# Loading and attending batch 0 in two row ranges, with fp32 rows below 256 by hardware DMA and a replanned opening

## Chip, cores, metric

One core of a Trainium2 chip (trn2). The metric is the device time of one execution in microseconds; medians over several runs are given. "Ratio" always means a kernel's time against the kernel before, run on the same chip in the same rounds.

## The reference, cut

Causal attention with 16 extra "beacon" keys and values that every query sees, then a two-layer feed-forward with ELU.

```python
B, H, S, Nb, D = 8, 8, 576, 16, 64          # all fp32
k_all = concat([beacon_k, k], axis=2); v_all = concat([beacon_v, v], axis=2)
scores = q @ k_all^T / 8;  causal mask on the S keys (beacons never masked)
a = softmax(scores);  attn = a @ v_all       # -> x: 4608 x 512
h = x @ w_in                                 # 512 x 2048
out = where(h > 0, h, exp(min(h, 0)) - 1) @ w_out
```

## The kernel before: the parts that matter here

The order of all instructions is written by hand for batches 0 to 2; a regular loop does the rest, one 512-token tile of the feed-forward beside the attention of one batch. Short names of the steps: `T` transposes q and k on TensorE, `cq`/`ck` copy them out, `S` a quarter of a head pair's scores, `x` their exponential on ScalarE, `m` the mask, `L` the row sums, `W` the value product, `n` the reciprocal by logarithm and exponential, `M` the scaling, `F` first matrix, `e r g` the ELU, `G` second matrix, `warm` multiplications of zeros that keep TensorE's clock up.

```python
# q and k: cast to bf16 by the software DMA queue (GpSimd), six rows per partition
def load_qk(b, h0, h1):
    for src, dst in ((q, st[b][0]), (k, st[b][1])):
        nc.gpsimd.dma_start(out=dst[:, h0:h1, :, :]..., in_=src[b, h0:h1, :, :]...)
# ... beacon keys on the two hardware queues
for b in range(B):
    (nc.sync if b % 2 == 0 else nc.scalar).dma_start(out=bk32[NB*b:NB*(b+1), :, :], in_=beacon_k[b]...)
# ... keys stand in chunks j of 128 rows; the last one has 80: kc = [128, 128, 128, 128, 80]
def quad(b, g, qa, qe, t, half, first):      # row sums (ones) or value product of four heads
    pcs = [...]                              # the pieces (chunk j, queries a to e, column c) of this query range
    for n, (j, a, e, c) in enumerate(pcs):
        for i in range(4):
            nc.tensor.matmul(out=t[32*i:32*(i+1), a-qa:e-qa],
                lhsT=ones[0:kc[j], :] if half is None else v16[0:kc[j], j, h, 32*half:32*(half+1)],
                rhs=ets[b, p][0:kc[j], i % 2, c:c+e-a], ...)
# ... four matmuls of one piece lie beside each other in four 32-column parts of the array
```

In batches 1 to 7, `L` and `W` of queries 0 to 511 call `quad` with five pieces, so a group of 20 matmuls; the last piece is chunk 4 with the 16 queries 496 to 511.

The softmax here doesn't subtract the row's maximum and nothing guards it: scores larger than these inputs give would overflow.

## Time and profile before

| | kernel before |
|---|---|
| median, 3 runs | 361.54 us (360.62 to 362.31) |
| profiled execution | 367.16 us, span on the core 365.5 us |
| TensorE busy | 96% of the span |

The profile's page gives busy times, then 40 equal slices; the chain of waits follows back from the last instruction what released each step. The lines are shown in the prediction. One number of the table deserved more attention than I gave it: the profiled execution took 5.6 us longer than the median.

### The profile page before, as it was taken

How to read it: one execution, taken by the hardware profiler on the slowest of the kernel's cores; microseconds unless marked ns; L12 is line 12 of the kernel's file. 1: busy time of each engine (PE TensorE's matmuls, PEld its weight loads, DVE VectorE, ACT ScalarE, POOL GpSimd, SP SyncE). 2: the span in 40 equal slices, each digit the busy share in tenths (PEclk: the TensorE clock that was granted, in tenths of full speed). 3: DMA queues.
4: the chain of work that ended last, by engine and by line, in shares of the span. 5: the costliest groups of instructions: out<-in, count | busy, mean ns of one | idle time of the engine just before them, and what ended most of it. 6: DMA issues, size and time to landing. Idle time of an engine off the chain costs nothing.

```text
span 365.5 us, 9406 instructions
## 1 busy us (share of the span) xinstructions
PE 350.7 (96%) x3944; PEld 172.6 (47%) x3944; DVE 252.8 (69%) x615; ACT 218.9 (60%) x345; POOL 97.8 (27%) x130
## 2 busy tenths in 40 slices
PE   7979999979999999999999999999999999999995
PEld 3546765533445444544454454445444444444442
DVE  3444883766987877777777878786868677677731
ACT  1997988665765776677566756776576433333300
POOL 8867447387194008400500050000000000000000
PEclk9997999998999999999999999999999999999999
DMA  8999999999999639973954294432000001001012
GB/s 119 170 197 168 181 200 146 102 162 152 169 92 152 83 102 96 164 82 90 100 67 60 61 117 76 64 63 63 29 32 30 30 30 57 29 30 58 29 64 81
DMA packets 124299, 34.69 MB, mean 95 GB/s; under 512 B 111969, under 2 KB 118625, under 8 KB 124257
## 3 DMA queue, kind: packets, MB, share of 16 engines
q0 software_dynamic: 93600, 18.49, 62.6%
q1 hardware_dynamic: 30080, 15.47, 21.6%
q8 instruction: 31, 0.51, 0.6%
q10 hardware_dynamic: 576, 0.13, 0.2%
q14 instruction: 12, 0.09, 0.1%
HBM read 37.22 MB, written 15.34 MB: 144 GB/s over the span
## 4 chain that ended last, share of the span: by engine, by line
PE 83%; ACT 9%; DVE 5%; issue 1%; DMA 1%; ACTq 0%; DVEq 0%
PE hps L434 34%; PE ops L465 32%; PE sc L278 7%; PE lt L315 5%; ACT et L288 3%; PE ut L315 3%; DVE xT L385 2%; ACT rl L351 1%; ACT rl L348 1%; DVE gt L456 1%; DMA bk_83<-in_beacon_k_dram 1%; DVE r L449 1%; ACT e L444 1%; ACT qk_97 L257 1%; PE w_161 L200 0%
## 5 line engine op out<-in xcount | busy, mean ns | idle before, releaser
L434 PE MATMUL hps<-xT,w_in_81 128*128 128x512 f16 (+1 forms) x640 | 151.1, 365 | 1.3 <-DVE gt L456 1.2
L465 PE MATMUL ops<-w_out_82,gt 128*128 128x512 f16 x576 | 145.3, 379 | 0.0
L444 ACT ACTIVATE e<-hps 128x512 f32<-128x512 f32 x144 | 85.4, 598 | 62.9 <-PE hps L434 62.4
L288 ACT ACTIVATE et<-sc 128x832 f16<-128x832 f32 x128 | 103.6, 873 | 17.6 <-PE sc L278 17.6
L456 DVE TENSOR_TENSOR gt<-hps,r 128x512 f16<-128x512 f32 x144 | 99.6, 691 | 5.4
L449 DVE TENSOR_SCALAR r<-e 128x512 f16<-128x512 f32 x144 | 65.3, 454 | 32.2 <-ACT e L444 30.8
L465 PEld LDWEIGHTS <-gt 128*128 128x128 f16 x576 | 55.8, 98 | 66.6 <-issue 0.6
L434 PEld LDWEIGHTS <-w_in_81 128*128 128x128 f16 x640 | 58.6, 99 | 60.6 <-issue 7.9
L304 DVE TENSOR_TENSOR et<-et,triu 128x256 f16<-128x256 f16 (+3 forms) x164 | 40.4, 270 | 27.9 <-ACT et L288 27.5
L472 DVE COPY osb<-ops 128x512 f32<-128x512 f32 x36 | 24.6, 682 | 10.2 <-PE ops L465 10.2
L494 POOL DMA_DIRECT2D qkd<-in_k_dram x20 | 20.2, 1362 | 3.7 <-DMA v_1733<-in_v_dram 2.4
L385 DVE TENSOR_TENSOR xT<-lt,rl 128x448 f16<-128x448 f32 (+6 forms) x28 | 10.6, 419 | 14.6 <-ACT rl L351 14.6
L494 POOL DMA_DIRECT2D qkd<-in_q_dram x20 | 18.8, 1053 | 3.8 <-DMA w_out_82<-in_moe_w_out_dram 3.4
L348 ACT ACTIVATE rl<-lt 128x512 f32<-128x512 f32 (+1 forms) x15 | 9.0, 603 | 16.7 <-PE lt L315 16.7
L348 ACT ACTIVATE rl<-ut 128x64 f32<-128x64 f32 x14 | 3.1, 223 | 23.0 <-DVE xT L385 23.0
L315 PEld LDWEIGHTS <-ones 128*32 128x32 f16 (+1 forms) x624 | 10.9, 97 | 8.7 <-issue 5.8
L351 ACT ACTIVATE rl<-rl 128x512 f32<-128x512 f32 (+2 forms) x30 | 13.8, 459 | 0.9
L385 DVE TENSOR_TENSOR xT<-ut,rl 128x448 f16<-128x448 f32 (+6 forms) x28 | 10.5, 416 | 4.5 <-PE ut L315 3.7
L200 PE MATMUL w_161<-zero 64*128 64x512 bf16 (+1 forms) x36 | 11.4, 440 | 1.3 <-DVE zero L152 1.3
L315 PE MATMUL lt<-et,ones 128*32 128x512 f16 (+7 forms) x320 | 12.3, 286 | 0.0
L140 POOL DMA_DIRECT2D w_in_81<-in_moe_w_in_dram x16 | 8.5, 542 | 4.2 <-DMA kst<-in_k_dram 1.0
L123 POOL DMA_DIRECT2D v_4331<-in_beacon_v_dram x1 | 0.5, 532 | 33.0 <-PE ut L315 33.0
(116 smaller groups left out, 221.7 us busy)
## 6 DMA issues: line engine op xcount, KB each, us to landing
...
```

The source lines that it names most:

```text
L278: nc.tensor.matmul(out=s[:, h, a - c0:e - c0], lhsT=t[D * h:D * (h + 1), 1, P * j:P * (j + 1)], rhs=t[D * h:D * (h + 1), 0, NB + qa + a - ...
L288: nc.scalar.activation(out=ets[b, p][:, :, GW * g:GW * (g + 1)], in_=sc[b, p, g][:, :, 0:GW], func=AFT.Exp, bias=0.0, scale=SCALE)
L304: nc.vector.tensor_tensor(out=o, in0=o, in1=triu[0:kc[j], :, t0:t0 + e - a], op=ALU.mult)
L315: nc.tensor.matmul(out=t[32 * i:32 * (i + 1), a - qa:e - qa], lhsT=ones[0:kc[j], :] if half is None else v16[0:kc[j], j, h, 32 * half:32 * ...
L385: nc.vector.tensor_tensor(out=x_tile(k)[:, cc, tok - TT * k:to - TT * k], in0=u[:, o:o + to - tok], in1=r[:, o:o + to - tok], op=ALU.mult)
L434: nc.tensor.matmul(out=h[:, n_, :], lhsT=w_in16[:, cc, P * fc:P * (fc + 1)], rhs=xt[k][:, cc, a - TT * k:e - TT * k], start=(cc == 0), sto ...
L444: nc.scalar.activation(out=eb[t, i], in_=flat(hp[t, i]), func=AFT.Exp, bias=0.0, scale=1.0)
L449: nc.vector.tensor_scalar(out=rb[t, i], in0=eb[t, i], scalar1=1.0, scalar2=1.0, op0=ALU.min, op1=ALU.subtract)
L456: nc.vector.tensor_tensor(out=flat(gt), in0=flat(hp[t, i]), in1=rb[t, i], op=ALU.max)
L465: nc.tensor.matmul(out=ob[t, tb_], lhsT=gts[t, fc][:, P * tb_:P * (tb_ + 1)], rhs=w_out16[:, fc, :], start=(fc == 0), stop=(fc == NFC - 1))
L472: nc.vector.tensor_copy(out=osb, in_=ob[t, tb_])
L494: nc.gpsimd.dma_start(out=st[b][i][s0:s0 + S // 4], in_=src[b, :, s0:s0 + S // 4].rearrange("h s d -> s h d"))
```

## The change

Its intent: rows 0 to 255 of batch 0 get their own loads, transposes and attention, so that the feed-forward can start on the first 256 tokens early. q and k below 256 come as fp32 over the hardware queues (no cast) and are transposed as fp32 matmuls against an identity; the rest follows as bf16 over the software queue. All copies of batch 0 go to VectorE, and the order of steps and loads is replanned. The core of the diff (cuts marked):

```diff
+    def load_qa(h0, h1):
+        for eng, src, dst in ((nc.sync, q, qa0[0]), (nc.scalar, k, qa0[1])):
+            eng.dma_start(out=dst[:, h0:h1, :, :]..., in_=src[0, h0:h1, 0:CUT, :]...)
+    def load_qb():                       # rows 256 and up, nc.gpsimd.dma_start, bf16
...
     for b in range(B):
         (nc.sync if b % 2 == 0 else nc.scalar).dma_start(out=bk32[...], in_=beacon_k[b]...)
+        if b in (1, 3):
+            load_qa(4 * (b // 2), 4 * (b // 2) + 4)
...
         for n, (j, a, e, c) in enumerate(pcs):
+            nk = min(kc[j], NB + e - P * j)
             for i in range(4):
                 nc.tensor.matmul(...
-                    lhsT=ones[0:kc[j], :] if half is None else v16[0:kc[j], j, h, ...],
-                    rhs=ets[b, p][0:kc[j], i % 2, c:c + e - a],
+                    lhsT=ones[0:nk, :] if half is None else v16[0:nk, j, h, ...],
+                    rhs=ets[b, p][0:nk, i % 2, c:c + e - a],
...
-    warm.12 bt bk cb.0.0 cb.0.3 cb.0.2 cb.0.1 cb.1.0 warm.3 T.0.0 cb.1.1 cb.1.3 cq.0.0 ck.0.0
+    warm.6 ld.qkA0 bt bk TA.0.0 cb.0.0 cb.0.1 cb.0.2 ld.qkA1 cb.0.3 cA.0.0 TA.0.1 TA.0.2 cb.1.0
... (the whole hand-written order is new)
```

`nk` is the number of key rows of a chunk that any of the piece's queries may see. Rows 0 to 255 need it, since only 16 rows of v's chunk 2 are loaded by then. But `quad` serves all batches: for chunk 4 and queries 496 to 511, `nk` is 16 where it was 80.

More of the change, by code (lines that the diff above doesn't have):

```diff
@@ L108, in new_stage @@
     def new_stage(b):
-        qst = stage.tile([PR, H, R, D], BF16, tag="qst")
-        kst = stage.tile([PR, H, R, D], BF16, tag="kst")
-        st.setdefault(b, [None] * 3)[0:2] = [qst, kst]
+        ts = [stage.tile([P, 2048], FP32, tag=tag, name=tag) for tag in ("qst", "kst")]
+        st.setdefault(b, [None] * 3)[0:2] = [
+            t[0:PR, 0:H * R * D // 2].bitcast(BF16).rearrange("p (h r d) -> p h r d", h=H, r=R) for t in ts]
     def load_qk(b, h0, h1):
@@ L118, in load_qk, with load_v @@
             )
-    def load_v(b, js):
+    RA, RB = CUT // P, 4
+    PB = (S - CUT) // RB
+    NA = H * RA * D
+    q0 = [stage.tile([P, NA + H * RB * D // 2], FP32, tag=tag, name=tag) for tag in ("qst", "kst")]
+    qa0 = [t[:, 0:NA].rearrange("p (h r d) -> p h r d", h=H, r=RA) for t in q0]
+    qb0 = [t[0:PB, NA:].bitcast(BF16).rearrange("p (h r d) -> p h r d", h=H, r=RB) for t in q0]
+    def load_qa(h0, h1):
+        for eng, src, dst in ((nc.sync, q, qa0[0]), (nc.scalar, k, qa0[1])):
+            eng.dma_start(
+                out=dst[:, h0:h1, :, :].rearrange("p h r d -> p h (r d)"),
+                in_=src[0, h0:h1, 0:CUT, :].rearrange("h (p r) d -> p h (r d)", r=RA))
+    def load_qb():
+        for src, dst in ((q, qb0[0]), (k, qb0[1])):
+            nc.gpsimd.dma_start(
+                out=dst.rearrange("p h r d -> p h (r d)"),
+                in_=src[0, :, CUT:S, :].rearrange("h (p r) d -> p h (r d)", r=RB))
+    def load_v(b, js, j_from=0, n_last=None):
         if js[0] == 0:
@@ L125, in load_v @@
         for j in js:
-            r0 = NB if j == 0 else 0
-            n = kc[j] - r0
+            r0 = NB if j == 0 else j_from if j == js[0] else 0
+            r1 = n_last if n_last and j == js[-1] else kc[j]
+            k0 = P * j - NB
             nc.gpsimd.dma_start(
-                out=st[b][2][r0:r0 + n, j, :, :],
-                in_=v[b, :, ilo[j]:ilo[j] + n, :].rearrange("h s d -> s h d"),
+                out=st[b][2][r0:r1, j, :, :],
+                in_=v[b, :, k0 + r0:k0 + r1, :].rearrange("h s d -> s h d"),
             )
@@ L159 @@
         nc.vector.memset(t[:, 1, SK:P * NKC], 0.0)
+    for t in qks[0:NP]:
+        nc.vector.memset(t[:, 1, NB + CUT:P * ((NB + CUT + P - 1) // P)], 0.0)
+    identf = konst.tile([P, P], FP32)
     identb = konst.tile([P, P], BF16)
     triu = konst.tile([P, 2, P], FP16)
-    bkst = konst.tile([P, H, D], BF16)
-    bkT = konst.tile([P, NP, P], BF16)
-    new_stage(0)
-    load_qk(0, 0, 2)
+    bkT = konst.tile([P, NP * P], BF16)
+    make_identity(nc, identf)
     make_identity(nc, identb)
-    load_qk(0, 2, 4)
     nc.gpsimd.memset(triu, 1.0)
@@ L173 @@
     )
-    load_qk(0, 4, 6)
-    load_qk(0, 6, 8)
-    new_stage(1)
-    load_v(0, [0, 1, 2])
-    load_v(0, [3, 4])
-    load_qk(1, 0, H // 2)
-    load_wi(0, 1024)
-    load_wi(1024, 2048)
-    load_qk(1, H // 2, H)
     op = {}
@@ L206, in bt @@
     def bt():
-        nc.vector.tensor_copy(out=bkst, in_=bk32)
-        tb.append(bank("hps", BF16, "tb"))
+        tb.append(bank("hps", name="tb"))
         for p in range(NP):
             nc.tensor.transpose(
-                out=tb[0][:, P * p:P * (p + 1)], in_=bkst[:, 2 * p:2 * p + 2, :], identity=identb)
+                out=tb[0][:, P * p:P * (p + 1)], in_=bk32[:, 2 * p:2 * p + 2, :], identity=identf)
     @step
     def bk():
-        nc.vector.tensor_copy(out=bkT, in_=tb[0][:, 0:NP * P])
+        nc.vector.tensor_copy(out=bkT, in_=tb[0])
@@ L217, with transposes @@
     tps, qkT, sc, ets = {}, {}, {}, {}
     seq = [0]
-    @step
-    def T(b, p):
-        if b == 0 and p < 3:
-            tps[b, p] = bank("hps", BF16, "tq"), bank("hps", BF16, "tk")
-            dsts = tps[b, p]
-        else:
-            tps[b, p] = psum.tile([P, 2, 1024], BF16, tag="S", name="tp")
-            dsts = tps[b, p][:, 0, :], tps[b, p][:, 1, :]
-        for dst, src in zip(dsts, st[b]):
-            for r in range(R):
-                for h in range(2):
-                    nc.tensor.transpose(
-                        out=dst[D * h:D * (h + 1), PR * r:PR * (r + 1)],
-                        in_=src[:, 2 * p + h, r, :],
-                        identity=identb[0:PR, 0:PR],
-                    )
+    def transposes(dsts, srcs, p, nr, w, ident):
+        for dst, src in zip(dsts, srcs):
+            for r in range(nr):
+                for h in range(2):
+                    o = dst[D * h:D * (h + 1), w * r:w * (r + 1)]
+                    x = src[:, 2 * p + h, r, :]
+                    if ident is identf:
+                        nc.tensor.matmul(
+                            out=o, lhsT=x, rhs=ident, start=True, stop=True, skip_group_check=True)
+                    else:
+                        nc.tensor.transpose(out=o, in_=x, identity=ident[0:w, 0:w])
@@ new lines, in halves, with TA, TB @@
+    def halves(t, n):
+        return t[:, 0:n], t[:, n:2 * n]
+    @step
+    def TA(b, p):
+        tps["A", p] = bank("hps", name="ta")
+        transposes(halves(tps["A", p], CUT), qa0, p, RA, P, identf)
+    @step
+    def TB(b, p):
+        tps["B", p] = psum.tile([P, 2, 1024], BF16, tag="S", name="tbb")[:, 0, :]
+        transposes(halves(tps["B", p], S - CUT), qb0, p, RB, PB, identb)
+    def T(b, p):
+        tps[b, p] = psum.tile([P, 2, 1024], BF16, tag="S", name="tp")
+        transposes((tps[b, p][:, 0, :], tps[b, p][:, 1, :]), st[b], p, R, PR, identb)
@@ L237, in cb, with cA, cB @@
+    op["T"] = T
+    @step
+    def cA(b, p):
+        nc.vector.tensor_copy(
+            out=qkT[b, p][:, :, NB:NB + CUT].rearrange("c i (p r) -> c i p r", r=RA),
+            in_=tps["A", p].rearrange("c (i r p) -> c i p r", i=2, r=RA))
+    @step
+    def cB(b, p):
+        nc.vector.tensor_copy(
+            out=qkT[b, p][:, :, NB + CUT:SK].rearrange("c i (p r) -> c i p r", r=RB),
+            in_=tps["B", p][:, 0:2 * (S - CUT)].rearrange("c (i r p) -> c i p r", i=2, r=RB))
     @step
@@ L240, in cb @@
         seq[0] += 1
-        nc.vector.tensor_copy(out=qkT[b, p][:, 1, 0:NB], in_=bkT[:, p, NB * b:NB * (b + 1)])
+        nc.vector.tensor_copy(out=qkT[b, p][:, 1, 0:NB], in_=bkT[:, P * p + NB * b:P * p + NB * (b + 1)])
     @step
@@ L251, in ck @@
             return
-        if b == 0 and p < 3:
-            nc.scalar.copy(
-                out=t[:, 1, NB:SK].rearrange("c (p r) -> c p r", r=R),
-                in_=tps[b, p][1][:, 0:S].rearrange("c (r p) -> c p r", r=R))
-        else:
-            nc.scalar.copy(
-                out=t[:, :, NB:SK].rearrange("c i (p r) -> c i p r", r=R),
-                in_=tps[b, p][:, :, 0:S].rearrange("c i (r p) -> c i p r", r=R))
-    @step
-    def cq(b, p):
-        nc.vector.tensor_copy(
-            out=qkT[b, p][:, 0, NB:SK].rearrange("c (p r) -> c p r", r=R),
-            in_=tps[b, p][0][:, 0:S].rearrange("c (r p) -> c p r", r=R))
+        nc.scalar.copy(
+            out=t[:, :, NB:SK].rearrange("c i (p r) -> c i p r", r=R),
+            in_=tps[b, p][:, :, 0:S].rearrange("c i (r p) -> c i p r", r=R))
     def S_(b, p, g):
@@ L316, in quad @@
                     out=t[32 * i:32 * (i + 1), a - qa:e - qa],
-                    lhsT=ones[0:kc[j], :] if half is None else v16[0:kc[j], j, h, 32 * half:32 * (half + 1)],
-                    rhs=ets[b, p][0:kc[j], i % 2, c:c + e - a],
+                    lhsT=ones[0:nk, :] if half is None else v16[0:nk, j, h, 32 * half:32 * (half + 1)],
+                    rhs=ets[b, p][0:nk, i % 2, c:c + e - a],
                     start=(first and n == 0), stop=(n == len(pcs) - 1), skip_group_check=True)
@@ L323, in L @@
     @step
-    def L(b, g):
-        if g == "A":
+    def L(b, *g):
+        if g[0] == "A":
             t = bank("ops", name="la")
@@ L330, in L @@
                 quad(b, i, 0, CUT, t[:, CUT * i:CUT * (i + 1)], None, i == 0)
-            lt[b, g] = t
-        elif g == "B":
-            t = psum.tile([P, 2, 512], FP32, tag="S", name="lt")
-            for i in range(2):
-                quad(b, i, CUT, S, t[:, i, 0:S - CUT], None, True)
-            lt[b, g] = t[:, :, 0:S - CUT]
+            lt[b, *g] = t
+        elif g[0] == "B":
+            t = lt[b, *g] = bank("ops", name="lb")[:, 0:S - CUT]
+            quad(b, g[1], CUT, S, t, None, True)
         else:
             t = psum.tile([P, 2, 512], FP32, tag="S", name="lt")
-            quad(b, g, 0, Q1, t[:, 0, :], None, True)
-            lt[b, g], ut[b, g, 0] = t[:, 0, :], t[:, 1, :]
+            quad(b, g[0], 0, Q1, t[:, 0, :], None, True)
+            lt[b, *g], ut[b, *g, 0] = t[:, 0, :], t[:, 1, :]
     @step
@@ L345, in n @@
         w = src.free_size()
-        rl = rls[b, *g] = attn.tile([P, 640], FP32, tag="rl", name="rl")
+        rl = rls[b, *g] = attn.tile([P, 512], FP32, tag="rl", name="rl")
         dst = rl[:, 0:w]
-        nc.scalar.activation(
-            out=dst.rearrange("p (g c) -> p g c", g=2) if len(src.shape) == 3 else dst,
-            in_=src, func=AFT.Ln, bias=0.0, scale=1.0)
+        nc.scalar.activation(out=dst, in_=src, func=AFT.Ln, bias=0.0, scale=1.0)
         nc.scalar.activation(out=dst, in_=dst, func=AFT.Exp, bias=0.0, scale=-1.0)
@@ L398, in M @@
             g, half = i
-            scale_out(b, 2 * g + half, CUT, S, ut[b, "B", g, half][:, 0:S - CUT],
-                      rls[b, "B"][:, (S - CUT) * g:(S - CUT) * (g + 1)])
+            scale_out(b, 2 * g + half, CUT, S, ut[b, "B", g, half][:, 0:S - CUT], rls[b, "B", g][:, 0:S - CUT])
         elif g == "R":
@@ L480, in wo, with ld @@
     @step
-    def wo(i):
-        load_wo(i)
+    def ld(x):
+        i = x[-1]
+        if x.startswith("win"):
+            load_wi(DF // 2 * int(i), DF // 2 * (int(i) + 1))
+        elif x.startswith("wo"):
+            load_wo(int(i))
+        elif x == "qk0B":
+            load_qb()
+        elif x == "v0A":
+            load_v(0, [0, 1, 2], n_last=NB)
+        elif x == "v0B":
+            load_v(0, [2, 3, 4], j_from=NB)
+        elif x.startswith("qk") and x != "qkA0" and x != "qkA1":
+            b = int(x[2])
+            if b not in st or st[b][0] is None:
+                new_stage(b)
+            load_qk(b, H // 2 * (i == "b"), H // 2 * (1 + (i == "b")))
+        elif x[0] == "v":
+            load_v(int(x[1]), list(range(NKC)))
     @step
     def lk(b):
-        if b < DB:
-            new_stage(b)
-            load_qk(b, 0, H)
-            return
-        st[b] = [None] * 3
+        st.setdefault(b, [None] * 3)
         for i, src in enumerate((q, k)):
@@ L504, in run @@
             f, *args = word.split(".")
-            op[f](*[a if a in "ABR" else int(a) for a in args])
+            op[f](*[int(a) if a.isdigit() else a for a in args])
     run("""
-    warm.12 bt bk cb.0.0 cb.0.3 cb.0.2 cb.0.1 cb.1.0 warm.3 T.0.0 cb.1.1 cb.1.3 cq.0.0 ck.0.0
-    warm.4.64 S.0.0.0 S.0.0.1 T.0.1 cb.1.2 x.0.0.0 cq.0.1 x.0.0.1 S.0.0.2 ck.0.1 x.0.0.2 warm.4.64
-    S.0.1.0 x.0.1.0 m.0.0.0 T.0.2 m.0.0.2 S.0.0.3 warm.1.64 S.0.1.1 x.0.0.3 x.0.1.1 warm.2.64 T.0.3
-    wo.0 wo.1 lv.1 lk.2 wo.2 wo.3 ck.0.2 cq.0.2 cb.2.3 warm.2.64 S.0.2.0 m.0.1.0 ck.0.3 warm.2.64
@@ L513 @@
-    S.0.3.0 x.0.2.0 m.0.0.3 m.0.2.0 warm.2.64 S.0.3.1 x.0.3.0 warm.2.64 S.0.2.1 x.0.3.1 warm.2.64
-    S.0.3.2 x.0.2.1 m.0.3.0 L.0.A S.0.3.3 x.0.3.2 cb.2.0 m.0.3.2 x.0.3.3 W.0.A.0 S.0.2.2 x.0.2.2
-    S.0.2.3 x.0.2.3 S.0.1.2 x.0.1.2 m.0.3.3 n.0.A T.1.0 T.1.1 W.0.A.1 cb.2.2 m.0.2.2 ck.1.0 m.0.2.3
-    m.0.1.2 ck.1.1 M.0.A.0 M.0.A.1 S.1.0.0 S.0.1.3 x.1.0.0 x.0.1.3 F.0.0 e.0.0 S.1.0.1 F.0.1 cb.2.1
-    m.1.0.0 x.1.0.1 m.0.1.3 S.1.0.2 r.0.0 L.0.B g.0.0 F.0.2 m.1.0.1 e.0.1 x.1.0.2 n.0.B r.0.1 g.0.1
@@ L518 @@
-    F.0.3 S.1.1.0 m.1.0.2 S.1.1.1 e.0.2 r.0.2 e.0.3 x.1.1.0 W.0.B.0.0 x.1.1.1 W.0.B.0.1 g.0.2
-    M.0.B.0.0 S.1.0.3 r.0.3 m.1.1.0 cb.3.2 m.1.1.1 F.0.7 T.1.2 M.0.B.0.1 x.1.0.3 T.1.3 e.0.7 g.0.3
-    F.0.6 r.0.7 ck.1.2 ck.1.3 g.0.7 m.1.0.3 e.0.6 F.0.4 S.1.3.0 r.0.6 e.0.4 S.1.1.2 W.0.B.1.0
-    x.1.3.0 W.0.B.1.1 lv.2 S.1.1.3 g.0.6 x.1.1.2 F.0.5 M.0.B.1.0 r.0.4 M.0.B.1.1 S.1.2.0 x.1.1.3
-    g.0.4 e.0.5 x.1.2.0 cb.3.1 S.1.2.1 m.1.3.0 m.1.1.3 F.1.0 e.1.0 m.1.1.2 G.0.0.0 r.0.5 m.1.2.0
-    g.0.5 r.1.0 S.1.3.1 F.1.1 x.1.2.1 x.1.3.1 e.1.1 S.1.3.2 S.1.3.3 g.1.0 m.1.2.1 F.1.2 x.1.3.2
@@ L524 @@
-    m.1.3.1 cb.3.0 r.1.1 g.1.1 x.1.3.3 e.1.2 G.0.0.1 m.1.3.2 S.1.2.2 S.1.2.3 m.1.3.3 r.1.2 F.1.3
-    x.1.2.2 cb.3.3 x.1.2.3 g.1.2 m.1.2.2 e.1.3 G.0.1.0 m.1.2.3 F.1.5 G.0.1.1 e.1.5 r.1.3 g.1.3 F.1.6
-    r.1.5 T.2.1 e.1.6 ck.2.1 T.2.0 g.1.5 F.1.7 S.2.1.0 ck.2.0 r.1.6 g.1.6 lk.3 S.2.0.0 G.0.0.2
-    x.2.1.0 m.2.1.0 x.2.0.0 S.2.0.1 S.2.0.2 G.0.1.2 m.2.0.0 x.2.0.1 x.2.0.2 L.1.0 W.1.0.0 m.2.0.1
-    m.2.0.2 T.2.2 n.1.0 ck.2.2 M.1.0.0 F.1.4 e.1.7 r.1.7 S.2.0.3 W.1.0.1 x.2.0.3 R.1.0 M.1.0.1 L.1.1
-    e.1.4 W.1.1.0 m.2.0.3 r.1.4 n.1.R.0 n.1.1 M.1.R.0 g.1.7 G.0.0.3 M.1.1.0 W.1.1.1 R.1.1 T.2.3
@@ L530 @@
-    G.0.1.3 o.0.0 M.1.1.1 n.1.R.1 ck.2.3 g.1.4 M.1.R.1 F.2.0 S.2.1.1 e.2.0 S.2.1.2 o.0.1 r.2.0 F.2.1
-    g.2.0 G.1.0.0 x.2.1.1 m.2.1.1 S.2.2.0 x.2.1.2 S.2.1.3 e.2.1 m.2.1.2 ck.3.2 x.2.2.0 x.2.1.3 F.2.3
-    G.1.0.1 r.2.1 g.2.1 F.2.5 S.2.3.0 m.2.2.0 e.2.3 m.2.1.3 r.2.3 x.2.3.0 L.2.0 lv.3 e.2.5 W.2.0.0
-    W.2.0.1 g.2.3 m.2.3.0 R.2.0 r.2.5 F.2.2 g.2.5 n.2.0 M.2.0.1 F.2.4 M.2.0.0 S.2.2.1 n.2.R.0 e.2.2
-    M.2.R.0 S.2.3.1 r.2.2 e.2.4 x.2.2.1 G.1.0.2 g.2.2 F.2.6 ck.3.0 r.2.4 s.0.1 m.2.2.1 x.2.3.1
@@ L535 @@
-    S.2.3.2 g.2.4 S.2.2.2 F.2.8 m.2.3.1 e.2.6 x.2.3.2 G.1.0.3 e.2.8 x.2.2.2 r.2.6 g.2.6 m.2.3.2
-    r.2.8 F.2.7 g.2.8 S.2.2.3 e.2.7 s.0.0 m.2.2.2 S.3.0.0 F.2.10 o.1.0 x.3.0.0 r.2.7 g.2.7 G.1.1.0
-    lk.4 e.2.10 m.3.0.0 r.2.10 ck.3.3 F.2.9 x.2.2.3 S.3.0.1 g.2.10 e.2.9 S.2.3.3 F.2.13 x.2.3.3
-    m.2.2.3 x.3.0.1 s.1.0 e.2.13 r.2.9 g.2.9 G.1.1.1 m.2.3.3 F.2.11 L.2.1 m.3.0.1 W.2.1.0 W.2.1.1
-    R.2.1 r.2.13 g.2.13 e.2.11 r.2.11 n.2.1 g.2.11 ck.3.1 F.2.12 M.2.1.1 M.2.1.0 F.2.14 n.2.R.1
-    S.3.0.2 e.2.12 M.2.R.1 e.2.14 r.2.12 S.3.0.3 g.2.12 r.2.14 g.2.14 x.3.0.3 G.1.1.2 m.3.0.3 F.2.15
@@ L541 @@
-    x.3.0.2 e.2.15 G.1.1.3 m.3.0.2 r.2.15 o.1.1 s.1.1 g.2.15
+    warm.6 ld.qkA0 bt bk TA.0.0 cb.0.0 cb.0.1 cb.0.2 ld.qkA1 cb.0.3 cA.0.0 TA.0.1 TA.0.2 cb.1.0
+    cb.1.1 cb.1.2 S.0.0.0 ld.qk0B ld.v0A cb.2.0 x.0.0.0 cA.0.1 S.0.1.0 TA.0.3 cA.0.2 S.0.2.0 m.0.0.0
+    cA.0.3 x.0.1.0 x.0.2.0 warm.1.64 TB.0.1 ld.win0 m.0.1.0 cB.0.1 S.0.3.0 m.0.2.0 x.0.3.0 m.0.3.0
+    warm.2.64 TB.0.0 S.0.1.1 L.0.A x.0.1.1 cB.0.0 n.0.A S.0.1.2 x.0.1.2 S.0.0.1 W.0.A.1 x.0.0.1
+    M.0.A.1 W.0.A.0 M.0.A.0 m.0.1.2 TB.0.2 F.0.0 S.0.0.2 ld.win1 F.0.2 cB.0.2 e.0.0 x.0.0.2 r.0.0
@@ new lines @@
+    g.0.0 S.0.0.3 S.0.1.3 m.0.0.2 e.0.2 F.0.1 x.0.0.3 r.0.2 ld.v0B x.0.1.3 S.0.2.1 g.0.2 ld.qk1a
+    F.0.3 cb.2.3 e.0.1 cb.2.1 m.0.0.3 m.0.1.3 r.0.1 S.0.2.2 L.0.B.0 x.0.2.1 x.0.2.2 TB.0.3 e.0.3
+    g.0.1 S.0.2.3 ld.wo0 m.0.2.2 F.0.4 cB.0.3 S.0.3.1 cb.3.3 x.0.2.3 n.0.B.0 S.0.3.2 r.0.3 W.0.B.0.1
+    g.0.3 F.0.5 ld.qk1b e.0.4 m.0.2.3 r.0.4 x.0.3.1 g.0.4 S.0.3.3 M.0.B.0.1 x.0.3.2 W.0.B.0.0
+    x.0.3.3 m.0.3.2 cb.1.3 ld.wo1 e.0.5 T.1.0 M.0.B.0.0 T.1.1 m.0.3.3 L.0.B.1 r.0.5 ck.1.0 ck.1.1
+    S.1.0.0 F.0.6 ld.qk2a g.0.5 F.0.7 x.1.0.0 e.0.6 n.0.B.1 m.1.0.0 r.0.6 g.0.6 S.1.1.0 S.1.1.1
@@ new lines @@
+    W.0.B.1.0 ld.wo3 ld.wo2 M.0.B.1.0 x.1.1.0 W.0.B.1.1 x.1.1.1 S.1.0.1 m.1.1.0 ld.v2 M.0.B.1.1
+    G.0.1.0 S.1.0.2 x.1.0.1 m.1.1.1 e.0.7 S.1.1.2 F.1.1 x.1.0.2 m.1.0.1 x.1.1.2 T.1.2 r.0.7 e.1.1
+    ck.1.2 g.0.7 T.1.3 m.1.0.2 F.1.3 G.0.0.0 m.1.1.2 ck.1.3 S.1.0.3 e.1.3 S.1.2.0 r.1.1 g.1.1 cb.3.2
+    x.1.0.3 x.1.2.0 F.1.0 r.1.3 g.1.3 S.1.2.1 m.1.0.3 x.1.2.1 e.1.0 G.0.1.1 S.1.1.3 S.1.2.2 m.1.2.0
+    F.1.2 m.1.2.1 x.1.1.3 x.1.2.2 cb.3.0 T.2.0 ck.2.0 S.1.2.3 r.1.0 G.0.0.1 S.1.3.0 G.0.1.2 x.1.2.3
@@ new lines @@
+    g.1.0 m.1.1.3 m.1.2.2 x.1.3.0 cb.2.2 S.1.3.1 m.1.2.3 ld.v1 e.1.2 m.1.3.0 r.1.2 g.1.2 x.1.3.1
+    S.1.3.2 F.1.5 G.0.1.3 x.1.3.2 S.2.0.0 m.1.3.1 e.1.5 m.1.3.2 S.1.3.3 x.2.0.0 o.0.1 G.0.0.2 r.1.5
+    g.1.5 S.2.0.1 x.1.3.3 G.0.0.3 S.2.0.2 x.2.0.1 ld.qk2b S.2.0.3 m.2.0.0 x.2.0.2 F.1.4 T.2.1
+    x.2.0.3 L.1.0 W.1.0.0 m.1.3.3 o.0.0 cb.3.1 ck.2.1 m.2.0.1 m.2.0.2 L.1.1 e.1.4 n.1.0 m.2.0.3
+    r.1.4 F.1.6 g.1.4 G.1.0.0 lk.3 M.1.0.0 W.1.0.1 e.1.6 R.1.0 W.1.1.0 n.1.1 r.1.6 F.1.7 g.1.6
+    M.1.0.1 n.1.R.0 G.1.1.0 M.1.1.0 M.1.R.0 S.2.1.0 e.1.7 ck.3.0 x.2.1.0 r.1.7 W.1.1.1 g.1.7 m.2.1.0
@@ new lines @@
+    R.1.1 G.1.0.1 S.2.1.1 M.1.1.1 n.1.R.1 M.1.R.1 F.2.0 x.2.1.1 S.2.1.2 S.2.1.3 lv.3 e.2.0 F.2.1
+    x.2.1.2 x.2.1.3 m.2.1.1 T.2.3 e.2.1 T.2.2 r.2.0 g.2.0 ck.2.3 F.2.2 ck.2.2 m.2.1.2 e.2.2 m.2.1.3
+    r.2.1 g.2.1 G.1.1.1 r.2.2 g.2.2 S.2.3.0 x.2.3.0 S.2.2.0 F.2.3 L.2.0 m.2.3.0 x.2.2.0 m.2.2.0
+    W.2.0.0 e.2.3 n.2.0 S.2.2.1 F.2.4 x.2.2.1 r.2.3 g.2.3 M.2.0.0 e.2.4 m.2.2.1 F.2.5 r.2.4 S.2.2.2
+    e.2.5 g.2.4 r.2.5 S.2.2.3 x.2.2.2 x.2.2.3 G.1.1.2 g.2.5 F.2.6 m.2.2.2 F.2.7 m.2.2.3 e.2.6
+    S.2.3.1 r.2.6 g.2.6 x.2.3.1 m.2.3.1 W.2.0.1 R.2.0 e.2.7 S.3.0.0 x.3.0.0 M.2.0.1 F.2.9 n.2.R.0
@@ new lines @@
+    r.2.7 g.2.7 G.1.0.2 e.2.9 F.2.8 M.2.R.0 S.2.3.2 e.2.8 S.2.3.3 m.3.0.0 r.2.9 g.2.9 r.2.8 x.2.3.2
+    G.1.1.3 g.2.8 F.2.10 F.2.12 x.2.3.3 e.2.10 m.2.3.2 e.2.12 S.3.0.1 o.1.1 m.2.3.3 L.2.1 r.2.10
+    W.2.1.0 ck.3.1 g.2.10 r.2.12 s.1.1 g.2.12 F.2.13 x.3.0.1 s.0.1 n.2.1 F.2.11 m.3.0.1 M.2.1.0
+    e.2.13 S.3.0.2 e.2.11 W.2.1.1 R.2.1 ck.3.2 r.2.13 g.2.13 x.3.0.2 F.2.14 S.3.0.3 r.2.11 e.2.14
+    g.2.11 m.3.0.2 M.2.1.1 n.2.R.1 G.1.0.3 r.2.14 g.2.14 M.2.R.1 x.3.0.3 ck.3.3 o.1.0 F.2.15 e.2.15
+    s.0.0 m.3.0.3 lk.4 s.1.0 r.2.15 g.2.15
```

## The prediction

> **What bounds the kernel now.** I read the page's busy shares and slices first, then the chain of waits, then TensorE's timeline of the opening, then stretches. Page of the kernel before (busy shares, then 40 slices of 9.1 us in tenths):
>
> ```profile
> PE 350.7 (96%) x3944; PEld 172.6 (47%) x3944; DVE 252.8 (69%) x615; ACT 218.9 (60%) x345; POOL 97.8 (27%) x130
> PE   7979999979999999999999999999999999999995
> ACT  1997988665765776677566756776576433333300
> PEclk9997999998999999999999999999999999999999
> DMA  8999999999999639973954294432000001001012
> ```
>
> TensorE is the bound over the whole span. Only the first three slices differ: there ScalarE is full and TensorE's busy time is partly padding. The DMA engines are at 9 for the first 120 us, so the order of loads matters. The chain that ended last (start, length, what):
>
> ```profile
> 2.23 3.93 DMA bk_83<-in_beacon_k_dram
> ...
> 9.76 1.62 ACT et L288 x2
> ...
> 11.90 3.04 ACT et L288 x4
> ...
> 16.50 6.82 ACT et L288 x9
> ...
> 27.08 1.82 PE hps L434 x8
> ...
> 80.14 2.94 issue
> 83.28 3.18 PE hps L434 x8
> ```
>
> Up to 6.2 us the end waits for the beacon keys, from 9.8 to 26.5 for ScalarE (all 16 exponentials of batch 0, its copies, then the logarithm and reciprocal, then two copies of batch 1), and from 27.0 for TensorE. At 80.14 TensorE stands still for 2.94 us though nothing that the profile shows is missing. TensorE's timeline:
>
> ```profile
> 6.88 0.40 PE L210 MATMUL tb<-identb,bkst 128*128 128x128 bf16 x4 [0.97 <-DVE bkst L207]
> ...
> 9.29 0.60 PE L278 MATMUL sc<-qk_96 64*128 64x256 bf16 x10
> ...
> 16.77 0.59 PE L200 MATMUL w_161<-zero 64*128 64x512 bf16 x2
> ...
> 27.01 1.89 PE L434 MATMUL hps<-xT,w_in_81 128*128 128x256 f16 x8
> ...
> 36.94 1.05 PE L434 MATMUL hps<-xT,w_in_81 128*128 128x256 f16 x8
> ```
>
> L200 multiplies zeros to keep the clock up. The first feed-forward matmul starts at 27.01, and the same eight matmuls take 1.89 us there and 1.05 us at 36.94: the clock is at half. Two stretches (length, busy time and count of each engine, clock, DMA share, GB/s):
>
> ```profile
> 27.00:106.20 79.20, 74.77 (x1145) 42.52 (x1143) 55.71 (x145) 59.90 (x93) 46.70 (x57) 0.94 1.76 152
> 106.00:143.20 37.20, 37.20 (x433) 17.59 (x432) 28.34 (x69) 24.38 (x41) 12.75 (x15) 1.00 1.12 111
> ```
>
> At 106.22 the regular loop (one 512-token tile per 37.2 us, TensorE always busy) begins. The edit doesn't touch it. So the whole question is when the tile after the hand-ordered part (call it F3) starts in the changed kernel: 106.22 us in the profiled run before.
>
> **What the Trainium skill says.** "TensorE: Matmul & The Clock Gate", Part 1: TensorE starts at half clock and gets the full one after about 3.4 us of sustained work. The trace agrees: the twelve opening fillers stand 0.42 us apart, later ones about 0.22. "FP8 and Floating Point Precision", TensorE Precision Notes: a true fp32 matmul takes four passes; the kernel before has none, so no trace shows it yet. "DMA: Bandwidth & Descriptors", Issuing engines are not separate DMA queues: loads issued from different engines interleave on the same 16 DMA engines. The DMA row fits. "Runtime: NRT & Kernel Launch", Instruction fetch mechanics: instructions are refilled in blocks of 256. The trace had recorded 2483 TensorE instructions when the stall at 80.14 began, near 2560, ten blocks; so I take it for a late refill, not a data wait.
>
> **The change, part by part.**
>
> *Columns.* Counting matmul columns in both instruction orders gives 1,062,400 before and 1,048,576 after: 27 fillers of 512 fall away (13,824). But the 36 fp32 matmuls (4,608 columns) count four times if they take four passes, which adds 3 x 4,608 = 13,824. TensorE's sum is therefore unchanged; fillers have become transposes. Any gain must come from less standing still and less half clock.
>
> *Start of the chain.* q and k rows below 256 are 1.05 MB of fp32 in 512-byte rows on the two hardware queues, in between the eight beacon loads. In the first 10 us before, 1152 hardware packets of 256 bytes or less took 13.4% of 160 us, 19 ns each; I choose 28 ns for 512 bytes. So 2048 x 28 + 1024 x 20 ns over 16 engines is about 4.9 us from 1.8 us on, plus about a microsecond to landing: the beacon keys land near 7.3 us (6.2 before). Then come 4 + 24 fp32 matmuls ahead of the first scores: 28 x 512 = 14,336 column passes, 6 us at full and 12 us at half clock if nothing overlaps, half of that for the 24 if the two 64-column halves overlap as the bf16 transposes do (24 in 0.56 us). With six fillers instead of twelve, and an idle stretch after them, they start cold. I take 6.5 us: first scores at 14, first exponential at 14.5 (9.76 before). This part loses almost 5 us.
>
> *What no longer stands in the way.* Rows 0 to 255 need only the first of four score groups of each pair, so the logarithm sits behind 5 exponentials instead of 16, and the eight copies of batch 0 leave ScalarE for VectorE. From the first exponential: five exponentials at 0.76 us paced by TensorE's remaining transposes, about 6 us; logarithm and reciprocal 1.15; two multiplies 1.3. The first feed-forward matmul can start at 14.5 + 8.5 = 23 (20 to 26), against 27.01. Its weights: half of them now come right behind 0.9 MB of SWDGE loads; before, they stood behind 2.3 MB. I expect them by about 20.
>
> *What has been pushed behind that point.* Before, 18 score groups and two batch-1 transposes had been done by then, after only 7 groups: 11 x 0.3 + 2 x 0.6 + 0.4 (last bf16 transposes) = 4.9 us more TensorE work behind it.
>
> *What the stretch behind it can save.* In 27 to 106.2 TensorE stood still for 79.20 - 74.77 = 4.4 us; a mean clock of 0.94 means 12% of it, 9.5 us, at half speed, 4.7 us lost. Together 9.1. The stall at 80 and its cold aftermath (3.25 us for eight matmuls worth 1.72) make 4.5 of these. The other 4.6 should go, as real work follows on real work. I give half of the 4.5 as saved, since the block boundary moves but DMA stays full. Against it I charge 1.5 us of new waits: ScalarE gets about 10 exponentials and two copies more behind the first feed-forward matmul, 59.9 + 7.6 + 2.1 = 70 us in some 75.
>
> *Sum.* 4.0 (earlier start) - 4.9 + 4.6 + 2.2 - 1.5 = 4.4 us, from 361.54 to **357 us**.
>
> **Rivals.** (a) *fp32 passes don't overlap and run cold*: first scores at 17 to 18 us, the feed-forward at 26; gain 0 to 1 us, time 361. For: four passes, fewer fillers, the idle stretch before. Against: the order was replanned with them in it. (b) *ScalarE becomes the bound from 14.5 on*: 76 us of work gives F3 no earlier than 91 even without a gap. With 10% gaps that is 99, still before TensorE's 102, so it costs waits, not the bound; time 358 to 360. (c) *Loads become the bound*: q and k of batch 2 and v of batch 1 now come late and in pieces; v of batch 1 is due only some 18 us of TensorE work after its buffer is free, and a v load took 11 to 12 us to land in the full stretch. If late, TensorE stops and goes cold; time 361 to 364. (d) *All works and the refill stall goes too*: no waits, no cold clock, 8 us gained, 353.
>
> **Range and chances.** The spread is mostly the start of the feed-forward (3 us either way), the stall (2) and new waits (2): about 4.5 us. Range 350.5 to 362.5. Faster by 2% needs less than 354.3, that is nearly all of (d): 0.27. Slower by 2% needs 368.8, which only a large load wait gives: 0.03. Within 2%: 0.70.
>
> **What would show it.** First exponential near 14.5 and first feed-forward matmul near 23; fp32 matmuls of about 0.1 us net each warm (0.2 if nothing overlaps); clock 1.0 from then to F3 but for one stall; F3 near 102; loop still 37.2 us per tile. The prediction is wrong if the opening's fp32 block ends well before 14 (then 353 or less) or TensorE waits for a load of batch 1 or 2 for several us (then 361 or more).

## The result, and the profile after

The changed kernel took **372.82 us** (371.92 to 376.25, 4 runs) against 361.65 us, ratio 1.0329 (95% interval 1.0258 to 1.0400). A later repeat (e12, 6 runs) gave 1.0266 (1.0211 to 1.0320). A ratio is the mean time of one kernel's fast runs over the mean of the other's of the same rounds, so it isn't quite the ratio of the medians. It is slower by about 3%.

Page of the changed kernel, busy shares and slices (now 9.3 us each):

```profile
PE 354.6 (96%) x3949; PEld 173.4 (47%) x3949; DVE 256.9 (69%) x623; ACT 216.3 (58%) x343; POOL 97.3 (26%) x129
PE   2699999999999999999999999999999999999996
ACT  1079999587775765577566755765657333333300
PEclk9999999999999999999999999999999999999999
DMA  8999999999999949963942296332000001001012
```

TensorE does almost nothing in the first slice, and ScalarE nothing in the second, though both are busy afterwards. The chain of waits in the opening (start, length, what):

```profile
1.73 4.36 DMA bk<-in_beacon_k_dram
6.11 6.38 DMA bk<-in_beacon_k_dram
...
12.85 1.08 PE tb L223 x4
13.93 4.33 PE ta L240 x48
...
26.62 1.05 PE hps L457 x8
```

A beacon load issued by 6.1 us is waited for until 12.49. The fp32 transposes (`ta`) take 4.3 us and the feed-forward starts at 26.62, where it started before. Which DMA queue worked from 7 to 13 us (packets, MB, time of the packets as a share of 16 engines; the times of transfers that overlap are all counted, so the sum passes 100% and a share isn't time that a queue had the engines for itself):

```profile
q0 software_dynamic: 3159, 0.91, 143.4%
q10 hardware_dynamic: 418, 0.13, 13.0%
q1 hardware_dynamic: 209, 0.05, 5.9%
```

From 2 to 7 us the hardware queues had moved 1.11 MB. Their last 627 packets, 0.13 MB, took until 12.49, while the software queue moved 0.91 MB. The second difference is in the regular loop. TensorE's timeline, three groups of 20 matmuls of a batch in the loop, first in the kernel before:

```profile
135.88 0.74 PE L315 MATMUL lt<-et,v_1733 128*32 128x512 f16 x20
136.47 0.74 PE L315 MATMUL ut<-et,v_1733 128*32 128x512 f16 x20
137.06 0.32 PE L315 MATMUL ut<-et,ones 128*32 128x64 f16 x20
```

and in the changed kernel, with its weight loads' timeline:

```profile
137.08 0.10 PEld L343 LDWEIGHTS <-ones 16*32 16x32 f16 x4 [0.17 <-issue]
...
137.20 0.86 PE L343 MATMUL lt<-et,v 128*32 128x512 f16 x20
137.99 0.86 PE L343 MATMUL ut<-et,v 128*32 128x512 f16 x20
138.79 0.33 PE L343 MATMUL ut<-et,ones 128*32 128x64 f16 x20
```

Read the starts: a group took 0.59 us and takes 0.79 to 0.80. Ahead of the weight load with 16 rows TensorE's loader stands idle for 0.17 us, with no data awaited. Each batch from 1 to 7 has six such groups: 42 in all.

### The profile page after: what moved, and what is told of

It is laid out like the page before. It is cut to its first block, busy times and chain, and to the rows that moved or that the text cites. A ratio compares the mean times of both kernels' runs of the same rounds, so it can differ in the third digit from the quotient of the medians.

```text
span 370.6 us, 9421 instructions
## 1 busy us (share of the span) xinstructions
PE 354.6 (96%) x3949; PEld 173.4 (47%) x3949; DVE 256.9 (69%) x623; ACT 216.3 (58%) x343; POOL 97.3 (26%) x129
## 4 chain that ended last, share of the span: by engine, by line
PE 88%; ACT 5%; DMA 3%; DVE 3%; issue 1%; SPq 0%; DVEq 0%; ACTq 0%
PE hps L457 33%; PE ops L488 33%; PE sc L305 7%; PE lt L343 6%; PE ut L343 5%; DMA bk<-in_beacon_k_dram 3%; ACT et L315 2%; PE ta L240 1%; ACT e L467 1%; PE tp L243 1%; ACT rl L374 1%; DVE xT L409 1%; DVE et L331 1%; PE ua L343 0%; ACT rl L375 0%
## 5 line engine op out<-in xcount | busy, mean ns | idle before, releaser
L457 PE MATMUL hps<-xT,w_in 128*128 128x512 f16 (+1 forms) x640 | 148.0, 359 | 0.9 <-DVE gt L479 0.4
L488 PE MATMUL ops<-w_out,gt 128*128 128x512 f16 x576 | 145.3, 379 | 0.0
L457 PEld LDWEIGHTS <-w_in 128*128 128x128 f16 x640 | 56.9, 98 | 58.9 <-issue 7.4
L331 DVE TENSOR_TENSOR et<-et,triu 128x256 f16<-128x256 f16 (+2 forms) x164 | 40.5, 270 | 23.8 <-ACT et L315 23.3
L150 POOL DMA_DIRECT2D v<-in_v_dram x41 | 35.6, 878 | 7.9 <-DMA w_out<-in_moe_w_out_dram 3.0
L305 PE MATMUL sc<-qk 64*128 64x208 bf16 (+9 forms) x528 | 36.2, 249 | 0.8 <-DVE xT L409 0.3
L305 PEld LDWEIGHTS <-qk 64*128 64x128 bf16 x528 | 18.4, 94 | 29.1 <-issue 24.5
L343 PEld LDWEIGHTS <-v 128*32 128x32 f16 (+1 forms) x1248 | 20.5, 94 | 12.8 <-issue 6.3
L343 PE MATMUL ut<-et,v 128*32 128x64 f16 (+6 forms) x840 | 19.0, 223 | 0.0
L343 PEld LDWEIGHTS <-ones 128*32 128x32 f16 (+2 forms) x624 | 10.3, 95 | 10.9 <-issue 7.9
```

The lines of the kernel that those rows point to most:

```text
L150: nc.gpsimd.dma_start(out=st[b][2][r0:r1, j, :, :], in_=v[b, :, k0 + r0:k0 + r1, :].rearrange("h s d -> s h d"),)
L305: nc.tensor.matmul(out=s[:, h, a - c0:e - c0], lhsT=t[D * h:D * (h + 1), 1, P * j:P * (j + 1)], rhs=t[D * h:D * (h + 1), 0, NB + qa + a - ...
L331: nc.vector.tensor_tensor(out=o, in0=o, in1=triu[0:kc[j], :, t0:t0 + e - a], op=ALU.mult)
L343: nc.tensor.matmul(out=t[32 * i:32 * (i + 1), a - qa:e - qa], lhsT=ones[0:nk, :] if half is None else v16[0:nk, j, h, 32 * half:32 * (half ...
L457: nc.tensor.matmul(out=h[:, n_, :], lhsT=w_in16[:, cc, P * fc:P * (fc + 1)], rhs=xt[k][:, cc, a - TT * k:e - TT * k], start=(cc == 0), sto ...
L488: nc.tensor.matmul(out=ob[t, tb_], lhsT=gts[t, fc][:, P * tb_:P * (tb_ + 1)], rhs=w_out16[:, fc, :], start=(fc == 0), stop=(fc == NFC - 1))
```

## The experiments

Two theories at first. **A**: the cut to 16 rows costs 0.20 us in each of 42 groups, 8.4 us. **B**: the late opening costs the time. In the table, "feed-forward" is the start of its first matmul, "loop" the start of the regular loop's first one, "rest" the span from there to the end; all from the one profiled execution. The ratio is against the kernel before.

| kernel | median us | ratio (95%) | feed-forward | loop | rest |
|---|---|---|---|---|---|
| before, first trace | 361.5 | 1 | 27.01 | 106.22 | 259.3 |
| before, second trace (e6) | 363.2 (one run) | - | 26.53 | 102.16 | 259.3 |
| changed, first trace | 372.8 | 1.0329 (1.0258 to 1.0400) | 26.62 | 106.80 | 263.8 |
| changed, second trace (e12) | 373.4 | 1.0266 (1.0211 to 1.0320) | 29.61 | 110.5 | 263.8 |
| e1 changed, full rows | 366.1 | 1.0090 (1.0065 to 1.0115) | 27.33 | 107.50 | 258.7 |
| e2 before, cut rows | 369.5 | 1.0146 (1.0090 to 1.0201) | 26.80 | 102.19 | 264.0 |
| e3 changed, beacons first | 369.8 | 1.0163 (1.0121 to 1.0206) | 24.54 | 104.30 | 263.7 |
| e4 = e1 + e3 | 362.8 | 0.9997 (0.9973 to 1.0021) | 23.69 | 102.85 | 258.7 |
| e10 = e1 + hold | 362.1 | 0.9981 (0.9960 to 1.0002) | 23.03 | 101.0 | 258.7 |
| e7 = e4 + hold | 360.5 | 0.9937 (0.9898 to 0.9976) | 19.05 | 100.1 | 258.7 |

Runs of the kernel before varied from 361.65 to 364.04 in the median over the sessions, so the ratios are what to compare.

### e1: full rows again in batches 1 to 7

```diff
-            nk = min(kc[j], NB + e - P * j)
+            nk = min(kc[j], NB + e - P * j) if b == 0 else kc[j]
```

> The changed kernel, but for batches 1 to 7 the last key chunk of every row-sum and value product is again contracted over its whole 80 rows instead of the 16 that the causal mask leaves. Theory A (the cut to 16 rows costs 0.20 us in each of 42 such groups, because the weight load of a 16-row matmul is no longer pulled ahead): 372.8 - 42 x 0.20 = 364.4 us, groups of 20 matmuls 0.60 us apart again, the regular loop at about 37.2 us per tile. Theory B (the late opening, beacon keys landing at 12.5 us, made the whole loss): stays at 372 to 373.

366.06 us, ratio 1.0090. The groups are 0.60 us apart again and the rest of the span fell from 263.8 to 258.7 us. Theory A's sign and most of its size hold: against the changed kernel's 1.0266 it gives back 1.8%, some 6.4 us, where 8.4 was expected. The loop's 30 groups show 5.1 us (0.17 each). The 12 in the hand-written part gain nothing in this trace, because it has a stall of 1.64 us and half clock behind it that the changed kernel's first trace lacks (see e12). In e4 and e10, which have the same edit and no such stall, TensorE is busy for 76.9 and 76.8 us from the first feed-forward matmul to the loop, against 78.9 in the changed kernel. Theory B alone falls.

### e2: the cut alone, in the kernel before

```diff
+            nk = min(kc[j], NB + e - P * j)
             for i in range(4):
...
-  lhsT=ones[0:kc[j], :] if half is None else v16[0:kc[j], j, h, ...],  rhs=ets[b, p][0:kc[j], ...]
+  lhsT=ones[0:nk, :] if half is None else v16[0:nk, j, h, ...],  rhs=ets[b, p][0:nk, ...]
```

> The kernel before, with nothing changed but that contraction cut (all batches, 42 + 6 groups). Theory A: 361.65 + 48 x 0.20 = 371 us, though up to 2 us of it may be hidden in the opening, so 369 to 371. Theory B: the same time as before, 361 to 362.

369.48 us, ratio 1.0146, 5.3 us. The opening is unchanged (loop at 102.19) and the rest is 264.0 instead of 259.3. So one line, which takes rows of zeros out of small matmuls, makes the kernel before slower by 1.5%. With e1's 0.9% for the opening the sum is 2.4%, and the changed kernel's repeat measured 2.7% (interval 2.1 to 3.2): the two causes add up.

### e3 and e4: the beacon loads first

```diff
-        if b in (1, 3):
-            load_qa(4 * (b // 2), 4 * (b // 2) + 4)
+    load_qa(0, 4)
+    load_qa(4, 8)          # after all eight beacon loads
```

> The changed kernel, with the eight beacon loads issued ahead of the four fp32 loads of q and k instead of between them. Theory B (late beacon keys are the main loss): beacon keys at about 5 us, first scores some 5 us earlier, time 366 to 368. Theory A: at most 3 us gained (372.8 to 370), because the fp32 rows are then what comes late behind the software queue, and w_in lands near 22 us anyway.

> Both edits. If the two causes add up: e1's time less what e3 gained, 360 to 363 us, that is about the time of the kernel before.

e3: 369.78 us, ratio 1.0163; about 3.7 us less than the changed kernel. The beacon keys' transposes start at 5.30 us instead of 12.85, but then the fp32 rows of k are what comes late. TensorE's timeline of e3:

```profile
6.32 1.12 PE L240 MATMUL ta<-identf,qst 128*64 128x128 f32 x8
10.85 1.12 PE L240 MATMUL ta<-identf,kst 128*64 128x128 f32 x8 [3.41 <-DMA kst<-in_k_dram]
```

e4: 362.84 us, ratio 0.9997. With both edits the changed kernel is level with the one before.

### e5: how many rows are cheap

```diff
+            if nk < kc[j] and b > 0:
+                nk = (16, 16, 32, 33, 48, 64, 65, 80)[b]    # batches 1 to 7: 16 to 80
```

> The changed kernel with another contraction length of the last key chunk in each batch (16, 32, 33, 48, 64, 65, 80 rows in batches 1 to 7; the rows beyond 16 hold masked zeros, so the result is the same). One look, read from the spacing of the groups of 20 matmuls. Theory A1 (a matmul of at most 32 rows puts the array into another tile size and switching costs): 0.80 us for 16 and 32, 0.60 from 33 on. A2 (any size but the full 128-row tile does, and 65 to 80 rows count as the full one): 0.80 up to 64 rows, 0.60 for 65 and 80. A3 (the fewer rows, the slower): a gradual change.

One look (372.78 us, single run). TensorE's timeline of batch 5 with 64 rows, then of batch 6 with 65:

```profile
216.31 0.87 PE L345 MATMUL lt<-et,v 128*32 128x512 f16 x20
217.11 0.87 PE L345 MATMUL ut<-et,v 128*32 128x512 f16 x20
217.91 0.33 PE L345 MATMUL ut<-et,ones 128*32 128x64 f16 x20
...
233.00 0.74 PE L345 MATMUL lt<-et,v 128*32 128x512 f16 x20
233.59 0.74 PE L345 MATMUL ut<-et,v 128*32 128x512 f16 x20
234.18 0.32 PE L345 MATMUL ut<-et,ones 128*32 128x64 f16 x20
```

0.80 us a group with 16, 32, 33, 48 and 64 rows, 0.59 with 65 and 80. It is a step, between 64 and 65, not a slope: A2. That fits the Trainium skill, "TensorEngine Tiling (Array Packing)", Tiling Modes: beside the modes of 128 rows there are modes of 64 and of 32 rows; and Key Properties: "Changing tiling mode (not just tile) drains the TensorE". The idle 0.17 us ahead of the weight load is consistent with such a drain; the trace doesn't name it.

### e6: the kernel before, a second trace

> The kernel before, once more, for a second trace. If the 2.9 us stall at 80 us and the half clock at 27 and 83 us belong to that one execution and not to the kernel, they are absent or elsewhere here, and the regular loop begins near 100 instead of 106.2 us. If they belong to the kernel, the same stall stands at the same instruction.

The same two stretches as in the prediction, in this trace (length; busy time and count of TensorE, its weight loads, VectorE, ScalarE, GpSimd; clock; DMA share; GB/s):

```profile
26.50:102.16 75.66, 72.42 (x1147) 41.96 (x1143) 56.39 (x145) 59.98 (x93) 46.83 (x57) 0.98 1.76 161
102.16:139.30 37.14, 37.13 (x433) 17.58 (x432) 28.42 (x68) 24.39 (x40) 12.71 (x15) 1.00 1.14 112
```

The span is 361.5 us and the loop begins at 102.16, 4.06 us earlier, with the rest the same 259.3. The mean clock is 0.98 instead of 0.94. The stall stands at the same instruction in both traces, ahead of the last three of 40 matmuls (TensorE's timeline, first trace, then e6):

```profile
83.08 0.21 PE L315 MATMUL ut<-et,v_953 80*32 80x64 f16 x3 [2.94 <-issue]
...
80.31 0.21 PE L315 MATMUL ut<-et,v 80*32 80x64 f16 x3 [0.99 <-issue]
```

So both of the expectation's cases are true in part: the stall's place belongs to the kernel, while its length and most of the half clock belonged to the one execution that I had read. Such an execution isn't rare: of 114 later runs of this kernel 14 were set aside as slow, at 365.8 us or more, and the profiled one took 367.16. Whether the stall makes them slow isn't known.

### e7 and e10: hold the software loads back

```diff
+    for _ in range(6):                       # dead writes: w_out16 is loaded much later
+        nc.gpsimd.memset(w_out16[:, NFC - 1, :], 0.0)
```

Six memsets on GpSimd, 3.4 us, ahead of its first load of batch 0. e7 is e4 with them, e10 is e1 with them (beacon loads still between the fp32 loads).

> e4 (full rows, beacons first) with six dead memsets on GpSimd that hold the first software loads back by some 3 us. If the software queue's packets are what make the fp32 loads of k late (first k transpose at 10.9 to 11.1 us in e3 and e4): all fp32 rows land by about 8 us, first scores at 12 to 13 instead of 15.3, first feed-forward matmul 0 to 2 us earlier (the weights, also held back, limit it), time 360 to 362.8. If the hardware queues are slow by themselves: k as late as in e4, everything 0 to 3 us later, 363 to 366.

> e1 (full rows, beacon loads between the fp32 loads as in the change) with the 3.4 us hold on the software loads. If it is the software queue's packets that starve the hardware queues, the hold alone brings the beacon keys from 12.2 to about 7 us whatever their place, and the time from e1's 366.1 to e7's 360.5. If the place of the beacon loads matters by itself, it stays at 363 or more.

e7: 360.52 us, ratio 0.9937. Queues from 4 to 8 us (packets, MB, share):

```profile
q10 hardware_dynamic: 1068, 0.53, 48.8%
q1 hardware_dynamic: 1034, 0.51, 43.5%
q0 software_dynamic: 45, 0.02, 11.1%
```

Alone, the hardware queues moved 1.04 MB in 4 us. The k transposes start at 7.61 us, the first exponential at 11.03 and the feed-forward at 19.05. TensorE then waits for the weights for 0.8 us, and later 2.1 us for a k load. e10: 362.09 us, ratio 0.9981, 1.1% less than e1. The beacon keys come in at 9.0 us there, not at 7, so it does less than e7 and its expectation was only half met. Both show by their landing times that it is the software queue's traffic that delays the hardware queues; the place of the beacon loads decides which of their loads suffers. How much of the time this makes is less sure: from e1's trace to e10's the feed-forward starts 4.3 us earlier, of which the beacon keys make 2.8, and 1.6 is e1's stall, which e10's trace doesn't have.

### e8, e9, e11: three refinements

e8 is e7 with ten opening fillers; e9 is e7 with 80 rows in batch 0's short chunk as well; e11 is e9 with four memsets.

```diff
-    warm.6 ld.qkA0 bt bk            # e8
+    warm.10 ld.qkA0 bt bk
-            nk = min(kc[j], NB + e - P * j) if b == 0 else kc[j]     # e9, e11
+            nk = min(kc[j], max(80, NB + e - P * j))                 # and v rows 16 to 79 of chunk 2 loaded early
```

> e7 with ten opening fillers instead of six, so that TensorE's clock is up when the fp32 transposes start. They take 0.21 us for a pair at half clock and 0.11 at full: up to 1.5 us less before the first scores than in e7, 0 to 1 us less in the time.

> e7, and in batch 0 too the short last chunk is contracted over 80 rows (the first v load fetches 80 rows of it instead of 16; the extra rows meet masked zeros). Six more groups lose their 0.20 us: 1.2 us if they all stand on the path, less 0.5 us for 512 more DMA packets ahead of the weights: 359.5 to 360.5, 0.8% under the kernel before. If weights are what the opening waits for, nothing is gained.

> e9 with four dead memsets instead of six, a hold of 2.3 us. Less delay for the weights that e7 waited 0.8 us for, but the last fp32 rows of k may again come late: 359 to 361, within 0.3% of e9.

Ratios 0.9919 (0.9887 to 0.9952), 0.9949 (0.9926 to 0.9973) and 0.9927 (0.9898 to 0.9956), medians 360.63, 360.86 and 359.74 us: none can be told from e7. In e8 the transposes did run at full clock, but TensorE then waited 2.3 us for the weights. In e9 the two value products of rows 0 to 255 took 0.97 instead of 1.68 us, but the expected 1.2 us don't show in the time. All of e7, e8, e9 and e11 beat the kernel before, by 0.5 to 0.8%.

### e12: the changed kernel again

> The changed kernel once more, for a ratio of as many runs as the others have. The first ratio, 1.033, came from four runs. If the two causes add, e1 (opening alone, 1.009) and e2 (row cut alone in the old opening, 1.0146) give 1.024, and the measured ratio should be 1.024 to 1.033; above 1.03 something is left over.

373.40 us, ratio 1.0266. The e1 and e2 shares sum to 1.024, inside its interval; nothing large is left over. Its trace, of an execution of 376.0 us, shows one thing that the first trace didn't:

```profile
29.05 0.36 PE L243 MATMUL tbb<-identb,qst 80*64 80x80 bf16 x5 [2.08 <-issue]
```

TensorE stands still in the middle of these eight transposes for 2.08 us with nothing awaited, and the feed-forward starts at 29.61 and at half clock. The traces of e1, e5 and e3 stand still at the same instruction for 1.64, 1.42 and 0.86 us; the first trace, e4 and e10 don't. So the starts in the table are good to some 3 us, and an unknown share of the opening's loss may be this stall and not late loads.

## Why the prediction was wrong

I predicted 357 us, a gain of 4.4; it was a loss of some 9 to 11.

- **"The edit doesn't touch it", said of the loop: wrong, and the largest single error.** The loop takes 38.3 us per tile instead of 37.2 (between the row-sum groups of one batch and the next in the regular loop: 114.94 to 153.28 us in the changed kernel, 114.36 to 151.59 before). I had read `nk` as something for batch 0 and counted matmul columns, in which the cut doesn't appear at all. e1 and e2 show it: 5.1 us in the rest of the span, 5.3 us in the time of e2. A matmul with fewer rows wasn't cheaper here (0.59 us a group with 65 and with 80 rows), and with 64 or fewer it was dearer.
- **"The beacon keys land near 7.3 us": wrong, 12.49.** The packet times were about right (e7 moved the same bytes by about 8 us, with the software loads held back). The sum had no term for the software loads, issued from 2.56 us on, on the same engines. I had put the first exponential at 14.5 and the feed-forward at 23; it became 18.60 and 26.62. So the "4.0 (earlier start)" of the sum was nothing: 26.62 against 26.53 in the second trace of before. With the loads landing as assumed (e7), the step does even more than I gave it, 19.05.
- **"4.9 us more TensorE work behind it": about right.** From the first feed-forward matmul to the loop TensorE was busy for 72.4 us before (e6) and 78.9 after, 6.5 more. Some 2 of these are the row cut in the 12 hand-ordered groups; without it e4 and e10 have 76.9 and 76.8, 4.4 to 4.5 more. The stretch itself grew from 75.6 to 80.2 us.
- **"4.6 and half of 4.5 saved": wrong, its base was not the kernel's usual state.** I charged the kernel with the stall and half clock of one profiled execution that was 5.6 us slower than the median. In e6's trace only 3.2 us of standing still and little half clock were left (in e2's, with the same opening, 2.4 us at clock 1.00), and the changed kernel's first trace, at clock 1.00, gains nothing that outweighs the pushed work.
- **The fp32 transposes: about right.** I took 6.5 us to the first scores, it was 5.35 (12.85 to 18.20). One of them (two matmul records in the trace, so x8 is four) takes 0.11 us in succession at full clock and 0.21 at half, my "about 0.1 us net each warm".
- **Rival (a): its numbers came true, its cause didn't.** It had the first scores at 17 to 18 us and the feed-forward at 26; they came at 18.20 and 26.62. But the passes did overlap; the beacon keys were late.
- **ScalarE as the new bound (rival b): refuted.** It was busy for 67.4 of 80.2 us in the same stretch and TensorE for 78.9, without new waits:

```profile
26.60:106.80 80.20, 78.94 (x1252) 43.78 (x1252) 61.06 (x158) 67.35 (x104) 46.41 (x56) 1.00 1.63 151
```

- **Rival (c) named loads as the danger, but the wrong ones**: those of batches 1 and 2, not the opening's own.
- **Slips in the working, too small to matter.** 1.8 + 4.9 + 1 is 7.7 us, not 7.3. By the order of steps 17 score groups, not 18, came before the first feed-forward matmul (4.6 us, not 4.9). The ninth slice of TensorE stands at 7 too, not only the first three; it is the stall. Of the twelve opening fillers the last two stand 0.21 to 0.24 us apart, not 0.42.

The sum corrected by these: -4.4 + 4.0 (no earlier start) + 5.3 (nothing net saved: 4.6 + 2.2 - 1.5) + 5.1 (the loop) = about +10 us, within what was measured.

Not settled: how much of the 0.6% that e7 gains would be left with bf16 transposes instead of fp32 ones, since no run changed that alone; whether the fp32 loads could be placed so that the weights aren't delayed at all; and how much of the opening's 0.9% in e1 is the stall of e12, since it comes and goes between executions.

## What to carry to other kernels

Read each line of a diff for every caller it reaches: a guard written for one batch changed 42 groups of matmuls in seven others. Don't cut the contraction of a few matmuls to 64 rows or fewer among full-height ones; multiplying masked zeros was 0.2 us a group cheaper. Loads that the first matmul waited for landed earlier with the DMA engines to themselves, so try issuing the other queue's bulk a little later; and before charging a kernel with a stall, see whether the profiled execution took as long as the others, and take a second trace.

## What the Trainium skill lacked or had wrong

- "TensorEngine Tiling (Array Packing)", Key Properties, says that a mode switch drains TensorE but gives no figure. Here a group of 20 matmuls whose last four had 16 to 64 rows, so a switch there and back if that is what it is, cost 0.20 us more than with 65 or 80 rows.
- "DMA: Bandwidth & Descriptors", Queues, rings and completion order, has engines alternate between the queues that have work. It doesn't say how late that can make a small load: in the changed kernel the last 0.13 MB of the two hardware queues, which TensorE waited for, took from 7 to 12.49 us beside 0.91 MB of the software queue. With the software queue held back they moved 1.04 MB in 4 us.
- "FP8 and Floating Point Precision", TensorE Precision Notes, gives four passes for a true fp32 matmul but no time. Here an fp32 transpose of 128 columns into 64 partitions took 0.11 us in succession at full clock and 0.21 at half, half of what a bf16 filler of 512 columns takes (0.21 to 0.24 and 0.43); why it isn't longer, the trace doesn't show.
- "Runtime: NRT & Kernel Launch", Instruction fetch mechanics, calls a block boundary mostly hidden. Here TensorE stood still, with nothing awaited, at fixed instructions and for a time that changed with the execution: in the kernel before after 2483 recorded instructions for 2.94 us in one trace and 0.99 in the next (e6), and in e6 and e2 after 1972, so 511 earlier, close to two blocks, for 0.66 and 0.83; in the changed kernel and its variants after 441 for 0 to 2.08 us. That a late refill is the cause was not tested.
